# The table that orders all 831 steps, made anew with other lengths for TensorE's work

## The chip, the core and the metric

The kernel runs on one core of a Trainium2 chip. The metric is the device time of one execution in microseconds (us), the median over runs. A core has five instruction queues that run beside each other and wait for one another by semaphores: PE (TensorE, matrix products; its weight loads are listed apart as PEld), DVE (VectorE), ACT (ScalarE), POOL (GpSimd) and SP, which here only issues transfers. A product writes into PSUM, and DVE or ACT must take it out before the PSUM buffer can be used again.

## What is computed

The reference is a gated recurrence over 768 time steps for 4 x 8 heads of 40 values, and a gated feed-forward layer with a mixing over time behind it. Cut to what matters:

```python
def _attn_ref(q, k, v, i_gate, f_gate, o_gate):      # q, k, v, o_gate: 4 x 8 x 768 x 40
    for t in range(S):
        m_new = np.maximum(f_gate[:, :, t] + m, i_gate[:, :, t])
        f_stab = np.exp(f_gate[:, :, t] + m - m_new)
        i_stab = np.exp(i_gate[:, :, t] - m_new)
        m = m_new
        C = f_stab[:, :, None, None] * C + i_stab[:, :, None, None] * np.einsum('bhd,bhe->bhde', vt, kt)
        n = f_stab[:, :, None] * n + i_stab[:, :, None] * kt
        h_tilde = np.einsum('bhde,bhe->bhd', C, qt)
        denom = np.maximum(np.abs(np.einsum('bhd,bhd->bh', n, qt)[:, :, None]), 1.0)
        y[:, :, t] = h_tilde / denom / (1.0 + np.exp(-o_gate[:, :, t]))

def _moe_ref(x, w_in, w_spatial, b_spatial, w_out):  # x: 4 x 768 x 320
    h = np.maximum(x @ w_in, 0.0)
    u, v = h[..., :512], h[..., 512:]
    v_n = (v - v.mean(-1)) / np.sqrt(v.var(-1) + 1e-06)
    v_s = np.einsum('ts,bsd->btd', w_spatial, v_n) + b_spatial[None, :, None]
    return (u * v_s) @ w_out
```

## The kernel before

The recurrence is cut into 24 packs, n = 0 to 23: four batches b of six packs, each of 128 time steps and all eight heads. A pack needs five groups of PE products: `pe_ex` (L364, one product, the gates' exponents), `pe_s` (L370, keys by queries), `pe_dc` (L379, what the pack adds to the state), `pe_intra` (L387, values within the pack) and `pe_inter` (L396, the carried state by the queries). The last four are packs of small products, 16 in the program and 32 instructions in the trace, that use the array as four 64x64 tiles. They are called pack groups here.

Around them stand, on DVE: `keys` (L415, weights times `pe_s`, frees its PSUM), `step` (L433, or L431 at a batch's start: the state, twice a pack), `rows` (L441 reads what `pe_inter` wrote, L445 what `pe_intra` wrote), `norm` (L451 to L459, ends in the tile x); on ACT: `weights` (L401) and `gate` (L410, L412); on POOL: `ktw` (L406), `decay` (L423, the state before each step) and `gated` (L465, L467). Then `turn` (L478) transposes x on PE into px, and `turn_h` (L484, ACT) and `turn_l` (L490, DVE) split it into a high and a low part, xH and xL.

The feed-forward layer takes products with 128 rows, in three terms of high and low parts. They are called large products here. `a_v` (L528) makes one pv tile for each of a batch's six 128-step blocks, by eight products of 512 columns; `ln1`, `ln2`, `ln3` (L535 to L559, on ACT, DVE and POOL) normalise it into vH and vL. `b_pu` (L570, eight products) and `b_pb` (L579 to L581, 18 products) make pu and pb for each of eight parts of a batch, and `b_g1` (L587 to L593) combines them on DVE and ACT. `c_out` (L603 to L605) is the last product.

Weights arrive as 64-bit numbers. `conv` (L261 to L283) makes 14 pieces of them into high and low 32-bit parts with work on ACT, DVE and POOL, and `split` (L296, L298) does the like for the spatial weights, six halves on DVE and six on POOL. They are wanted by the large products, and their steps stand among the packs of the first batch.

The program builds a list `stages` of 831 generators in a plain order (packs, conversions, products). Each generator yields between its instructions. What order the instructions get on all five queues, and which PSUM and SBUF buffers follow each other, is set by a table of 2534 numbers: each number takes the next step of that generator.

```python
    gens = [steps(*s) for s in stages]
    for k in ORDER or [k for k in range(len(gens)) for _ in range(99)]:
        next(gens[k], None)
```

Each engine then works through its own queue in that order and never skips ahead of an instruction that waits. PSUM holds four buffers for ex, px, pv, pu, pb and pc in rotation, and one double buffer each for SX (`pe_s` and `pe_inter`) and DX (`pe_dc` and `pe_intra`).

Of the kernel before, what the change touches and what calls it, by code (L numbers as in the profile page):

```python
# [37 lines left out]
def mlstm_moe(ctx: ExitStack, tc: tile.TileContext, a):  # L38
# [806 lines left out]
    def steps(f, args):  # L845
        r = f(*args)
        if r is not None:
            yield from r
# [4 lines that stand above are left out]
# [73 lines left out]
```

## Time and profile before

| what | us |
|---|---|
| median of 3 runs | 376.23 |
| lowest and highest of them | 375.11, 378.67 |
| the profiled execution's own time | 378.9 |
| its span, first to last instruction | 377.1 |
| PE busy in the span | 330.6 |
| PE weight loads busy | 298.9 |
| DVE, ACT, POOL busy | 220.1, 144.8, 111.7 |

The profile's page cuts the span into 40 equal slices of 9.4 us and gives each engine's busy tenths, then lists groups of instructions and the waits behind them. A row of a timeline has start, duration, engine, source line, operation, output and input, and in brackets how long the engine stood idle before it and what ended that. Matmuls overlap: their durations are longer than the distance from one to the next, and the distance is what PE pays. In the rows for stretches, "PEclk" is the TensorE clock that was granted, as a share of full speed.

### The profile page before, as it was taken

The page shows a single profiled execution, that of the slowest core. Times are in us where ns is not written, and L with a number is a line of the kernel's source. Part 1 is how long each engine was busy: PE and PEld are TensorE (multiplying, and loading weights), DVE is VectorE, ACT ScalarE, POOL GpSimd, SP SyncE. Part 2 cuts the span into 40 slices and gives each one's busy share as a digit, 9 for nine tenths or more (in the row PEclk, how much of TensorE's full clock was granted, in tenths as well). Part 3 has the DMA queues.
Part 4 walks back from the last instruction along what each step waited for, and adds up shares of the span by engine and source line. Part 5 has one row for each costly group of instructions (what it writes and reads, how often), then busy time and mean ns, then how long its engine had stood idle before and what let it go on. Part 6 is the DMA issues. An engine that isn't in the chain of part 4 may idle for free.

```text
span 377.1 us, 10595 instructions
## 1 busy us (share of the span) xinstructions
PE 330.6 (88%) x4426; PEld 298.9 (79%) x4426; DVE 220.1 (58%) x552; ACT 144.8 (38%) x335; POOL 111.7 (30%) x178
## 2 busy tenths in 40 slices
PE   0215685989699999999999999999999999999996
PEld 0104574756678899989899999889899998999996
DVE  6556869569779877345767454447675234614231
ACT  6256214267624332367332322663321216701211
POOL 5156645256535244111423232123331101200000
PEclk9999999989869999999999999999999999999999
DMA  7856244554251324300233414002100100100101
GB/s 200 253 155 224 82 127 138 161 171 128 67 170 55 127 86 145 105 2 18 78 94 123 142 56 141 1 20 73 56 2 2 54 1 0 54 0 0 51 5 52
DMA packets 16047, 32.24 MB, mean 85 GB/s; under 512 B 4028, under 2 KB 8920, under 8 KB 16000
## 3 DMA queue, kind: packets, MB, share of 16 engines
q1 hardware_dynamic: 15456, 31.30, 27.3%
q8 instruction: 35, 0.57, 0.6%
q0 software_dynamic: 416, 0.15, 0.2%
q10 hardware_dynamic: 128, 0.12, 0.1%
q14 instruction: 12, 0.10, 0.1%
HBM read 27.19 MB, written 4.33 MB: 84 GB/s over the span
## 4 chain that ended last, share of the span: by engine, by line
PE 80%; DVE 7%; DMA 5%; POOL 3%; issue 2%; SPq 1%; ACT 1%; POOLq 0%; DVEq 0%; ACTq 0%
PE pv L528 12%; PE pu L570 12%; PE pb L579 10%; PE pb L581 9%; PE pb L580 9%; PE DX L387 4%; PE SX L396 4%; PE pc L603 4%; PE pc L605 4%; PE pc L604 4%; PE SX L370 3%; PE px L478 3%; DMA w<-in_w_in 2%; PE DX L379 2%; DMA QK<-in_qk 2%
## 5 line engine op out<-in xcount | busy, mean ns | idle before, releaser
L579 PE MATMUL pb<-wsH,vH 128*128 128x384 f32 x192 | 69.0, 359 | 0.7 <-DVE g L587 0.7
L580 PE MATMUL pb<-wsL,vH 128*128 128x384 f32 x192 | 65.2, 339 | 0.0
L581 PE MATMUL pb<-wsH,vL 128*128 128x384 f32 x192 | 65.0, 339 | 0.0
L591 ACT CAST big<-g 128x384 fp32r<-128x384 f32 x32 | 16.4, 513 | 95.3 <-DVE g L589 93.2
L587 DVE TENSOR_TENSOR g<-pb,bsp 128x384 f32<-128x384 f32 x32 | 17.8, 556 | 43.0 <-PE pb L581 42.7
L579 PEld LDWEIGHTS pb<-wsH,vH 128*128 128x128 f32 x192 | 36.3, 189 | 2.6 <-DVE g L587 1.0
L580 PEld LDWEIGHTS pb<-wsL,vH 128*128 128x128 f32 x192 | 36.5, 190 | 0.2
L581 PEld LDWEIGHTS pb<-wsH,vL 128*128 128x128 f32 x192 | 36.4, 190 | 0.0
L545 POOL TENSOR_TENSOR st<-st,half_neg 128x1 f32<-128x1 f32 x24 | 14.7, 619 | 67.5 <-DVE st L543 64.5
L570 PE MATMUL pu<-xH,wiH 128*128 128x384 f32 x96 | 33.1, 345 | 0.4 <-DVE xL L490 0.4
L423 POOL TENSOR_TENSOR ST<-ST,DEC 104x164 f32<-104x164 f32 x40 | 21.9, 548 | 37.5 <-DVE ST L433 24.7
L528 PE MATMUL pv<-wiH,xH 128*128 128x512 f32 x72 | 30.0, 428 | 0.0
L603 PE MATMUL pc<-woH,big 128*128 128x320 f32 x96 | 29.8, 311 | 0.0
L605 PE MATMUL pc<-woH,big 128*128 128x320 f32 x96 | 29.6, 308 | 0.0
L604 PE MATMUL pc<-woL,big 128*128 128x320 f32 x96 | 29.6, 308 | 0.0
L387 PEld LDWEIGHTS DX<-RH,KS 64*64 64x64 f32 x768 | 15.6, 154 | 13.8 <-DVE ST L433 7.6
L387 PE MATMUL DX<-RH,KS 64*64 64x41 f32 x768 | 18.6, 248 | 8.8 <-DVE ST L433 6.9
L401 ACT ACTIVATE W<-ex 128x512 f32<-128x512 f32 x24 | 14.3, 595 | 31.2 <-PE ex L364 19.0
L406 POOL TENSOR_TENSOR RH<-RH,W 128x320 f32<-128x320 f32 x24 | 17.7, 738 | 28.4 <-ACT W L401 27.7
L370 PE MATMUL SX<-QK 40*64 40x64 f32 x768 | 20.9, 258 | 5.1 <-DVE KS L415 4.7
L484 ACT ACTIVATE xH<-px 128x384 fp32r<-128x384 f32 x24 | 11.8, 490 | 34.4 <-PE px L478 34.3
L415 DVE TENSOR_TENSOR KS<-SX,W 128x512 f32<-128x512 f32 x24 | 16.5, 686 | 14.5 <-PE DX L387 9.5
(120 smaller groups left out, 766.3 us busy)
## 6 DMA issues: line engine op xcount, KB each, us to landing
RH<-in_vk SPq DMA_DIRECT2D x24, 484.0 KB
QK<-in_qk SPq DMA_DIRECT2D x48, 160.0 KB
out<-ot SPq DMA_DIRECT2D x24, 160.0 KB
big<-in_w_sp SPq DMA_DIRECT2D x6, 384.0 KB
w64b<-in_w_out SPq DMA_DIRECT2D x4, 320.0 KB
w<-in_w_in SPq DMA_DIRECT2D x4, 256.0 KB
w64b<-in_w_in SPq DMA_DIRECT2D x4, 256.0 KB
w<-in_w_rem SPq DMA_DIRECT2D x2, 256.0 KB
```

Source lines behind the costliest of these rows:

```text
L370: nc.tensor.matmul(s_[half(e ^ hf), hf, j * L:(j + 1) * L], QK[feat(hf), e, 0, j], QK[feat(hf), e, 1, j], start=True, stop=True)
L387: nc.tensor.matmul(intra_[half(e), hf, j * E:(j + 1) * E], ks[r, h], rh_v(rh)[r, h], start=True, stop=True)
L423: nc.gpsimd.tensor_tensor(out=ST[(2 * n + e + 1) % NST][0:HI], in0=state(n, e)[0:HI], in1=DEC[0:HI, 2 * k + e, b * HH:(b + 1) * HH].unsque ...
L528: nc.tensor.matmul(pm, l, r, start=i == 0, stop=i == len(terms) - 1)
L570: nc.tensor.matmul(pu, w, x, start=i == 0, stop=i == len(terms) - 1)
L579: nc.tensor.matmul(pb, vH[:, cd], wsH[hf][:, s], start=s == 0, stop=False)
L580: nc.tensor.matmul(pb, vH[:, cd], wsL[hf][:, s], start=False, stop=False)
L581: nc.tensor.matmul(pb, vL[:, cd], wsH[hf][:, s], start=False, stop=s == NB - 1)
L587: nc.vector.tensor_tensor(out=g, in0=pb_[(b, hf, d)], in1=bsp[:, hf * 384:hf * 384 + 384], op=ALU.add)
L603: nc.tensor.matmul(pc, gH[:, c], woH[:, d], start=d == 0, stop=False)
L604: nc.tensor.matmul(pc, gH[:, c], woL[:, d], start=False, stop=False)
L605: nc.tensor.matmul(pc, gL[:, c], woH[:, d], start=False, stop=d == 3)
```

## The change

Nothing but the table is different. The 831 stages, their code, their tiles and the number of instructions that do arithmetic stay as they are; the list is a new sequence of the same 2534 numbers. It was made with measured lengths of the pack groups in PE's two clock states, and of the changes between pack groups and large products. A line of it:

```diff
-ORDER = [5, 0, 0, 0, 16, 16, 2, 0, 4, 8, 9, 6, 28, 1, 7, 16, 18, 0, 42, 11, 3, 10, 14, 0, 18, 18, 12, 0, 20, 15,
...
+ORDER = [16, 16, 0, 0, 16, 0, 0, 1, 9, 3, 7, 4, 27, 0, 50, 18, 5, 13, 8, 0, 2, 12, 10, 0, 0, 18, 18, 15, 6, 20,
...
```

What it moves is seen in the queues. Three places on PE follow, before and after. In the names, SX and DX are the two PSUM buffers; the line tells the group. QK_108 and QK_109 hold the keys and queries of packs 6 and 7.

The first place is around packs 3 to 6. PE's queue before, from `pe_intra` of pack 3 to the first rows of `pe_inter` of pack 4:

```order
L387 MATMUL DX<-RH_105,KS_101 64x41 x16
L478 MATMUL px<-ident,x 128x128 x3
L364 MATMUL ex<-GM_76,AT_75 128x512
L379 MATMUL DX<-RH_103 40x41 x8
L387 MATMUL DX<-RH_102,KS_100 64x41 x16
L370 MATMUL SX<-QK_108 64x64 x16
L478 MATMUL px<-ident,x 128x128 x3
L396 MATMUL SX<-ST_114,QK_106 64x41 x2
```

The same place after:

```order
L379 MATMUL DX<-RH_102 40x41 x16
L387 MATMUL DX<-RH_105,KS_101 64x41 x16
L370 MATMUL SX<-QK_108 64x64 x16
L396 MATMUL SX<-ST_114,QK_106 64x41 x2
L396 MATMUL SX<-ST_115,QK_106 64x41 x2
```

`pe_s` of pack 6 and `pe_inter` of pack 4 moved ahead of two transposes, `pe_dc` of pack 5 and `pe_intra` of pack 4. On DVE, `keys` of pack 5, which frees SX for them, moved ahead of x of pack 3.

The second place is where the first large products begin. PE's queue before, from the end of the second pv tile:

```order
L528 MATMUL pv<-wiH,xL 128x512
L528 MATMUL pv<-wiH,xH 128x512
L528 MATMUL pv<-wiL,xL 128x512
L364 MATMUL ex<-GM_77,AT_75 128x512
L379 MATMUL DX<-RH_104 40x41 x16
L370 MATMUL SX<-QK_109 64x64 x16
L387 MATMUL DX<-RH_103,KS_101 64x41 x16
```

The same groups after, in the first pv tile:

```order
L528 MATMUL pv<-wiH,xH 128x512
L370 MATMUL SX<-QK_109 64x64 x16
L528 MATMUL pv<-wiL,xH 128x512
L528 MATMUL pv<-wiH,xL 128x512
L528 MATMUL pv<-wiH,xH 128x512
L528 MATMUL pv<-wiL,xL 128x512
L379 MATMUL DX<-RH_104 40x41 x16
L396 MATMUL SX<-ST_111,QK_107 64x41 x2
```

`pe_s` of pack 7 and `pe_dc` of pack 6 moved from behind both pv tiles to within and behind the first one, ahead of `pe_inter` of pack 5. Four products of the second tile then stand ahead of `pe_intra` of pack 5, and four behind it.

The third place is around `pe_intra` of pack 7 (DX from RH_105). PE's queue before:

```order
L364 MATMUL ex<-GM_77,AT_73 128x512
L570 MATMUL pu<-xH,wiL 128x384
L570 MATMUL pu<-xL,wiH 128x384
L570 MATMUL pu<-xH,wiH 128x384
L570 MATMUL pu<-xL,wiL 128x384
L379 MATMUL DX<-RH_102 40x41 x16
L387 MATMUL DX<-RH_105,KS_101 64x41 x16
L396 MATMUL SX<-ST_115,QK_109 64x41 x2
```

The same place after:

```order
L528 MATMUL pv<-wiL,xL 128x512
L379 MATMUL DX<-RH_102 40x41 x16
L579 MATMUL pb<-wsH_93,vH 128x384
L580 MATMUL pb<-wsL_95,vH 128x384
L581 MATMUL pb<-wsH_93,vL 128x384
L387 MATMUL DX<-RH_105,KS_101 64x41 x16
L579 MATMUL pb<-wsH_93,vH 128x384
L580 MATMUL pb<-wsL_95,vH 128x384
```

Three products of the first pb tile moved in between `pe_dc` of pack 8 and `pe_intra` of pack 7, and `pe_inter` of pack 7 moved ahead of both.

2 lines of the change are left out of this document (1 added, 1 removed).

## The prediction, made before the changed kernel ran

> **What bounds the kernel now.** I read the page's slices first, then the stretches, then who waits for whom, then the timeline at the places where a wait is long.
>
> ```profile
> PE   0215685989699999999999999999999999999996
> DVE  6556869569779877345767454447675234614231
> ```
>
> PE is full from the twelfth slice on (9.4 us each, so from about 112 us) and half empty before. DVE is busiest in the slices where PE is not full. The stretches say it in numbers; columns are span, PE, PE weight loads, DVE, ACT, POOL, granted clock, DMA share, GB/s:
>
> ```profile
> 30.70:62.20 31.50, 21.19 (x590) 17.77 (x590) 24.51 (x57) 12.12 (x28) 18.00 (x27) 1.00 0.44 131
> 62.20:77.60 15.40, 14.41 (x228) 10.96 (x228) 8.27 (x23) 4.54 (x11) 4.30 (x7) 1.00 0.47 142
> 77.60:83.30 5.70, 3.93 (x72) 2.93 (x72) 4.30 (x14) 4.49 (x13) 3.79 (x6) 0.70 0.70 229
> 83.30:96.50 13.20, 12.85 (x147) 9.64 (x143) 12.60 (x31) 9.52 (x25) 8.68 (x13) 1.00 0.33 92
> 96.50:100.30 3.80, 0.70 (x45) 0.58 (x46) 3.49 (x11) 2.02 (x4) 1.95 (x4) 1.00 0.28 51
> 100.30:110.60 10.30, 10.30 (x207) 9.12 (x204) 5.96 (x18) 4.48 (x11) 3.73 (x7) 0.50 0.48 150
> 110.60:112.00 1.40, 1.40 (x9) 1.24 (x8) 1.40 (x3) 0.00 (x0) 1.07 (x1) 1.00 0.77 302
> 112.00:370.00 258.00, 256.92 (x3080) 239.69 (x3080) 140.92 (x359) 90.81 (x206) 57.14 (x92) 1.00 0.18 55
> ```
>
> The reader is to see two regimes. From 112 to 370 us PE is busy 256.92 of 258.00 us at full clock: only less PE work helps there. From 30.7 us (the first `keys`) to 112.0 us (the end of the first pb tile) PE and DVE take turns waiting. DVE is busy 24.51 + 8.27 + 4.30 + 12.60 + 3.49 + 5.96 + 1.40 = 60.5 of 81.3 us, idle 20.8. PE runs part of the time at half clock: 0.50 in 100.3 to 110.6. The clock of 1.00 shown before 77 us is not to be believed, since the products themselves are slow there:
>
> ```profile
> 75.13 0.63 PE L528 MATMUL pv<-wiH,xH 128*128 128x512 f32 x1
> 75.56 0.63 PE L528 MATMUL pv<-wiL,xL 128*128 128x512 f32 x1
> 84.30 0.39 PE L528 MATMUL pv<-wiH,xH 128*128 128x512 f32 x1
> 84.53 0.40 PE L528 MATMUL pv<-wiL,xH 128*128 128x512 f32 x1
> ```
>
> Starts are 0.43 us apart at 75 us and 0.23 at 84. So PE is at half clock until about 76.5 us; these are its two states.
>
> **The marker.** Both tables put exactly the same PE work ahead of the 18th and last product of the first pb tile: packs up to `pe_s` of 10 and `pe_dc` of 9, six pv tiles, two pu tiles. Before, that product ends at 112.0 us. Since PE never waits behind it, the change is worth the shift of this marker, plus what PE's work behind it gains or loses.
>
> **Term 1, conversions come earlier: +4.7 us on DVE.** Ahead of the first `b_g1`, DVE now has more `conv` work: about two further pieces of w_out. Their rows:
>
> ```profile
> L272 DVE SCALAR_TENSOR_TENSOR bitsb<-w64b,bitsb 128x320 f32<-128x320 uint32 x4 | 3.2, 803 | 0.0
> L263 DVE TENSOR_SCALAR bitsb<-bitsb 128x320 int32<-128x320 int32 x4 | 2.8, 696 | 0.0
> L265 DVE SCALAR_TENSOR_TENSOR bitsb<-w64b,bitsb 128x320 int32<-128x320 int32 x4 | 2.0, 497 | 0.0
> L283 DVE TENSOR_TENSOR woL<-bitsb 128x320 fp32r<-128x320 f32 x4 | 1.9, 478 | 0.0
> L270 DVE TENSOR_SCALAR bitsb<-bitsb 128x320 int32<-128x320 int32 x4 | 1.3, 320 | 0.0
> ```
>
> Twice (0.80 + 0.50 + 0.48 + 0.32) and once 0.70 is 4.9 us, less 0.2 for a `rows` that now follows and a `step` that now precedes: 4.7. This work isn't new, it leaves the stretch behind the marker, where DVE has room (140.92 of 258). Bounds: 0 if all of it falls into DVE's idle time, 4.7 if none does; I count it in full and the idle time apart. The splits and the later w_in pieces move further, from between packs 5 to 8 to between packs 2 to 5, but stay on the same side of the marker.
>
> **Term 2, DVE's waits: -10.5 us.** What DVE waited for between 30.7 and 112.3 us, the four longest:
>
> ```profile
> DVE xs L441 <- PE SX L370: 6.3, 2, 4.7
> DVE x L459 <- PE px L478: 2.6, 2, 2.2
> DVE KS L415 <- PE SX L396: 2.5, 1, 2.5
> DVE KS L415 <- PE DX L387: 1.9, 2, 1.1
> ```
>
> (a) The 2.5 us are `keys` of pack 6, held up by `pe_inter` of pack 4 behind a transpose:
>
> ```profile
> 65.82 0.90 PE L478 MATMUL px<-ident,x 128*128 128x128 f32 x3
> 66.65 1.09 PE L396 MATMUL SX<-ST,QK 40*64 40x41 f32 x32
> 67.91 0.69 DVE L415 TENSOR_TENSOR KS<-SX,W 128x512 f32<-128x512 f32 x1 [2.46 <-PE SX L396]
> ```
>
> In the new queue `pe_inter` of pack 4 stands four groups earlier, and `keys` waits for `pe_intra` of pack 4 alone. Bounds 0 to -2.5; I take -2, since the waits for `pe_intra` in the list are about 1 us at most and partly there already.
>
> (b) The 4.7 us are `rows` of pack 5. `pe_inter` of pack 5 was done early, but DVE was kept from SX until `pe_s` of pack 7, which stood behind the second pv tile:
>
> ```profile
> 71.38 1.09 PE L396 MATMUL SX<-ST,QK 40*64 40x41 f32 x32
> 76.87 0.67 PE L370 MATMUL SX<-QK 40*64 40x64 f32 x32
> 77.60 0.50 DVE L441 TENSOR_TENSOR xs<-SX,ET 128x328 f32<-128x328 f32 x1 [4.67 <-PE SX L370]
> ```
>
> Now `pe_s` of pack 7 stands ahead of `pe_inter` of pack 5. What is late next: that `pe_inter` stands behind half a pv tile (four products of 0.43 us, 1.7 us), and x of pack 5 behind the rest of the second tile and a transpose. Bounds 0 to -4.7; I take -2.5.
>
> (c) The worst stall of PE comes after the clock has risen:
>
> ```profile
> 96.51 0.52 PE L379 MATMUL DX<-RH 64*40 64x41 f32 x32
> 99.76 0.31 DVE L433 TENSOR_TENSOR ST<-DX,ST 104x164 f32<-104x164 f32 x1
> 100.12 0.95 PE L387 MATMUL DX<-RH,KS 64*64 64x41 f32 x32 [3.10 <-DVE ST L433]
> ```
>
> `pe_intra` of pack 7 waited 3.10 us for the first `step` of pack 8, which stood in DVE's queue behind the normalisation of three blocks. Behind this gap the clock fell to 0.50 for 10.3 us. PE was the bound there: DVE idled 10.30 - 5.96 = 4.3 us. The new order puts three pb products into the gap, and has the normalisations earlier in DVE's queue against PE, because (a) and (b) bring DVE forward. I expect a gap of about 1 us, and no fall. The 4.3 us then go to about 1: -3.5 (bounds 0 to -4.3).
>
> (d) In 30.7 to 62.2 us DVE idled 31.5 - 24.5 = 7.0 us in many short waits. The pieces and splits moved in between the packs fill some: -2.5 (bounds 0 to -7.0).
>
> Together -2 - 2.5 - 3.5 - 2.5 = -10.5, half of the 20.8.
>
> [...]
>
> **Term 3, changes on PE behind the marker: -0.7 us.** What a pack group costs among large products:
>
> ```profile
> 120.86 0.34 PE L581 MATMUL pb<-wsH,vL 128*128 128x384 f32 x1
> 121.13 0.68 PE L387 MATMUL DX<-RH,KS 64*64 64x41 f32 x32
> 121.74 0.44 PE L579 MATMUL pb<-wsH,vH 128*128 128x384 f32 x1
> 122.02 0.33 PE L580 MATMUL pb<-wsL,vH 128*128 128x384 f32 x1
> 122.19 0.34 PE L581 MATMUL pb<-wsH,vL 128*128 128x384 f32 x1
> ```
>
> Large products start 0.17 apart (122.02 to 122.19). Entering takes 0.27 and the first product behind takes 0.28, so about 0.1 + 0.1 are lost at each end of a run, and up to 0.1 more inside. Behind the marker the old queue has 29 runs of pack groups between large products, the new one 27, and four fewer places where a transpose adjoins a group: 2 x 0.2 to 0.3 plus 4 x about 0.05, say -0.7. So little, because lengths and changes were already roughly served.
>
> **What else moves.** SP now issues the last three transfers of spatial weights ahead of those for RH of pack 5, instead of at 73 us; at 131 GB/s used in that stretch against 229 in a later one there is room, and I cost it at nothing. If not, `ktw` of pack 5 is late next. POOL gets two splits ahead of `decay` of pack 4; POOL's 18.00 of 31.50 us leave room, and its cost is nothing unless that `decay` is late for `step`.
>
> **The sum.** 4.7 - 10.5 - 0.7 = -6.5 us. On the profiled execution, 378.9, that is 372.4; on the median, 376.23, it is 369.7. The profiled one lies 2.7 above the median, perhaps with a longer fall of the clock than others, which would make (c) smaller for them; the choices in (a) to (d) lie in the middle of their bounds. I predict 369.7.
>
> **Rivals.**
> - More of the waiting goes: the bounds of (a) to (d) add up to -18.5; if -15.5 of it goes, 376.2 + 4.7 - 15.5 - 0.7 = 364.7. For it: all three long waits lose their cause at once. Against: each has a next one behind it.
> - The waits only change place: DVE idles as long as the added work is, so -4.7, and the marker stays: 376.2 - 0.7 = 375.5. For it: PE and DVE depend on each other at every group, and the half clock slows both. [...]
> - DVE is the bound, and the conversions delay the state. If none of DVE's 20.8 us of idle time goes, the marker is 4.7 us later: 376.2 + 4.7 - 0.7 = 380.2, slower. For it: DVE is busy 12.60 of 13.20 us in 83.3 to 96.5. Against: its longest wait had nothing to do with DVE's load. It decides from an idle time that shrinks by less than 4.0 us.
>
> **How the numbers follow.** A measurement of this kernel can tell about 1% from no change. The forecast has a chance of 0.45 (366.5 to 372.5), the first rival 0.18, the second 0.24, the third 0.13. Faster by over 1% (below 372.5): 0.63. Within 1%: 0.25. Slower: 0.12. The range from 363.5 to 377.0 leaves out about 2 in 10, on the rivals' far sides.
>
> **What would show it.** The last product of the first pb tile ends at about 105.5 us (before 112.0). `rows` of pack 5 waits under 3 us. No stall of PE above 2 us between 84 us and the marker, and no half clock there. DVE idles about 10 us between the first `keys` and the marker. Behind it PE stays busy over 99%, with 27 runs. I am wrong if the marker is at 110 or later, if the clock falls once more, or if PE waits for DVE behind the marker.

## The result, and the profile after

The changed kernel takes 364.24 us (median of 4 runs, 364.11 to 364.68), the kernel before, run beside it, 375.67 us (4 runs, 374.69 to 378.67). The ratio is 0.9685, with a 95% interval of 0.9628 to 0.9742. The profiled execution of the changed kernel took 364.34 us, its span is 362.5. The forecast was 369.7 in a range of 363.5 to 377.0: the sign is right, the size is that of the first rival (364.7).

The page's slices (9.1 us each) of the changed kernel, PE, DVE and the granted clock:

```profile
PE   1123764999999999999999999999999999999996
DVE  6668999799988861447587273565844435533131
PEclk9999999999999999999999999999999999999999
```

PE is full from the eighth slice on, before from the twelfth. In slices 4 to 14 DVE's digits are 8 or 9 but for one 7; before they went down to 5. PEclk counts the time before the trace's first clock record as full speed, which it isn't: products of 512 columns start 0.42 us apart at 70.25 us and 0.23 apart at 72.34.

For the stretches I cut both kernels at the same work: first `keys`, first product of the first pv tile, the marker (last product of the first pb tile), last products. Columns as in the prediction: span, then busy time of PE, PE weight loads, DVE, ACT and POOL, granted clock, DMA share, GB/s. The stretches of the kernel before:

```profile
0.00:30.74 30.74, 5.15 (x44) 3.50 (x44) 17.69 (x42) 15.03 (x38) 13.07 (x26) 1.00 0.74 216
30.74:67.67 36.93, 25.73 (x705) 21.64 (x705) 27.72 (x64) 13.97 (x32) 20.90 (x31) 1.00 0.45 133
67.67:112.16 44.49, 39.21 (x578) 30.60 (x574) 32.94 (x88) 23.18 (x58) 20.63 (x29) 0.85 0.45 137
112.16:374.00 261.84, 260.48 (x3104) 243.15 (x3103) 141.79 (x360) 92.38 (x210) 57.14 (x92) 1.00 0.17 54
```

The same stretches of the changed kernel:

```profile
0.00:31.13 31.13, 5.25 (x44) 3.51 (x44) 20.75 (x49) 17.52 (x44) 13.79 (x27) 1.00 0.76 221
31.13:69.67 38.54, 26.03 (x705) 21.73 (x706) 34.51 (x74) 15.70 (x35) 24.69 (x35) 1.00 0.53 165
69.67:99.80 30.13, 29.98 (x576) 23.36 (x574) 28.56 (x82) 19.70 (x50) 16.30 (x24) 1.00 0.46 138
99.80:360.00 260.20, 259.16 (x3104) 243.20 (x3103) 139.82 (x350) 91.60 (x208) 56.88 (x92) 1.00 0.18 56
```

The marker moved from 112.16 to 99.80 us, 12.36 earlier. All of that comes from one stretch, from the first pv tile to the marker: 44.49 us became 30.13. The packs ahead of it even take 1.61 us longer (36.93, 38.54). In the stretch that gained, PE idled 5.28 us before and 0.15 after (span less busy time), which is 5.13 of the 14.36 us; the other 9.23 is the same work done in less busy time, 29.98 us in place of 39.21. The clock can account for all of it. Before, PE was at half clock there until 76.46 and in two falls later:

```profile
76.46:79.87 3.41, 1.58 (x97) 1.37 (x96) 2.04 (x5) 3.17 (x8) 1.97 (x3) 1.00 0.49 147
79.87:83.28 3.41, 3.41 (x52) 2.40 (x44) 2.26 (x9) 2.22 (x7) 2.03 (x4) 0.50 0.73 247
96.94:100.35 3.41, 0.31 (x26) 0.23 (x16) 3.10 (x10) 1.69 (x3) 1.56 (x3) 1.00 0.30 56
100.35:103.76 3.41, 3.41 (x99) 3.29 (x92) 1.80 (x4) 2.48 (x7) 1.68 (x3) 0.50 0.32 129
```

These are windows of 3.41 us. Behind a window in which PE idled 1.83 us (3.41 - 1.58) follows one at 0.50; behind one with 3.10 us idle follow three (to 110.59). In the changed kernel the products of the first pv tile show when the clock rises, and no record shows it falling before the end:

```profile
70.25 0.63 PE L528 MATMUL pv<-wiL,xH 128*128 128x512 f32 x1
72.34 0.39 PE L528 MATMUL pv<-wiH,xL 128*128 128x512 f32 x1
```

Full speed begins at 70.98 by the trace's clock records, 1.31 us behind the start of that tile (69.67); before, it was 8.79 us (67.67 to 76.46). So 8.79 + 13.65 = 22.4 us at half clock became 1.3. Half of the difference, 10.6 us (an estimate, by the products' starts of 0.42 and 0.23 us apart), bounds what the clock can have given; 9.23 were seen.

The waits of DVE, 31 to 100 us, of the changed kernel (total, times, longest):

```profile
DVE x L459 <- PE px L478: 1.9, 2, 1.7
DVE KS L415 <- ACT W L401: 1.1, 2, 0.6
DVE KS L415 <- PE DX L387: 0.6, 2, 0.4
```

The wait of `rows` for `pe_s` (6.3 us before) is gone from the list. From the first `keys` to the marker DVE idles 38.54 - 34.51 + 30.13 - 28.56 = 5.60 us, before 9.21 + 11.55 = 20.76.

Not all went well. PE's waits from 31 to 360 us in the changed kernel begin with one of 5.3 us, and PE's longest wait behind the first `keys` was 3.1 before:

```profile
PE SX L370 <- DVE KS L415: 6.2, 2, 5.3
PE DX L379 <- POOL RH L406: 4.7, 1, 4.7
```

DVE and POOL at the place of the 5.3 us, changed kernel (start, duration):

```profile
59.46 3.44 DVE L272 SCALAR_TENSOR_TENSOR bitsb<-w64b,bitsb 128x256 f32<-128x256 uint32 x1
62.83 0.49 DVE L445 TENSOR_TENSOR xs<-DX,xs 128x328 f32<-128x328 f32 x1
63.24 0.68 DVE L415 TENSOR_TENSOR KS<-SX,W 128x512 f32<-128x512 f32 x1
59.42 1.01 POOL L298 TENSOR_TENSOR wsL<-big,wsH 128x384 fp32r<-128x384 f32 x1
60.37 0.88 POOL L467 TENSOR_TENSOR x<-RH,x 128x320 f32<-128x320 f32 x1
61.18 0.76 POOL L406 TENSOR_TENSOR RH<-RH,W 128x320 f32<-128x320 f32 x1
61.88 0.74 POOL L280 TENSOR_TENSOR bitsb<-bitsb,wiH 128x256 f32<-128x256 f32 x1
```

A step of conv 8 (L272) that takes 0.42 us in other places took 3.44, just while POOL worked without a break, and `rows` and `keys` of the next packs stood behind it. This is the change's own new cost, and it lies in the stretch that got longer.

### The profile page after: what moved, and what is told of

It is laid out like the page before. It is cut to its first block, busy times and chain, and to the rows that moved or that the text cites. A ratio compares the mean times of both kernels' runs of the same rounds, so it can differ in the third digit from the quotient of the medians.

```text
span 362.5 us, 10599 instructions
## 1 busy us (share of the span) xinstructions
PE 320.4 (88%) x4426; PEld 291.8 (80%) x4426; DVE 223.7 (62%) x552; ACT 144.5 (40%) x335; POOL 111.7 (31%) x178
## 4 chain that ended last, share of the span: by engine, by line
PE 77%; DMA 8%; DVE 7%; issue 3%; ACT 2%; POOL 1%; SPq 1%; ACTq 0%; DVEq 0%; POOLq 0%
PE pu L570 12%; PE pv L528 10%; PE pb L579 10%; PE pb L581 9%; PE pb L580 9%; PE pc L603 4%; PE pc L605 4%; PE pc L604 4%; DMA QK<-in_qk 4%; PE DX L387 3%; PE SX L396 3%; PE SX L370 3%; PE px L478 2%; DMA RH<-in_vk 2%; PE DX L379 2%
## 5 line engine op out<-in xcount | busy, mean ns | idle before, releaser
L579 PE MATMUL pb<-wsH,vH 128*128 128x384 f32 x192 | 67.8, 353 | 0.2 <-DVE g L587 0.2
L370 PE MATMUL SX<-QK 40*64 40x64 f32 x768 | 20.1, 250 | 15.4 <-DMA QK<-in_qk 8.0
L370 PEld LDWEIGHTS SX<-QK 40*64 40x64 f32 x768 | 16.6, 159 | 18.2 <-DMA QK<-in_qk 8.2
L528 PE MATMUL pv<-wiH,xH 128*128 128x512 f32 x72 | 28.7, 408 | 0.1
L593 DVE TENSOR_TENSOR big<-g,big 128x384 fp32r<-128x384 f32 x32 | 18.6, 581 | 12.3 <-ACT big L591 12.3
L406 POOL TENSOR_TENSOR RH<-RH,W 128x320 f32<-128x320 f32 x24 | 18.8, 781 | 19.0 <-ACT W L401 18.7
L465 POOL TENSOR_TENSOR x<-RH,x 128x64 f32<-128x64 f32 x24 | 9.1, 380 | 48.4 <-DVE x L459 45.5
```

The source lines that it names most:

```text
L370: nc.tensor.matmul(s_[half(e ^ hf), hf, j * L:(j + 1) * L], QK[feat(hf), e, 0, j], QK[feat(hf), e, 1, j], start=True, stop=True)
L406: nc.gpsimd.tensor_tensor(out=kt, in0=kt, in1=Wt[n][:, :, L - 1:L].broadcast_to([128, H, D]), op=ALU.mult)
L528: nc.tensor.matmul(pm, l, r, start=i == 0, stop=i == len(terms) - 1)
L579: nc.tensor.matmul(pb, vH[:, cd], wsH[hf][:, s], start=s == 0, stop=False)
L593: nc.vector.tensor_tensor(out=gL, in0=g, in1=gH.bitcast(F32), op=ALU.subtract)
```

## The experiments

Four questions: which part of the list brings the gain (e1, e2); whether single waits of the kernel before explain it (e3 to e6); what a stall costs in the changed kernel (e12); and whether the 3.44 us and DVE's load ahead of the first pv tile are real costs (e7 to e11). All were timed beside the kernel before, whose medians in the four sessions were 377.68, 377.43, 377.64 and 376.33 us.

| run | median us | ratio to before, 95% |
|---|---|---|
| e1_new_head | 368.50 | 0.9665 to 0.9798 |
| e2_new_tail | 378.29 | 0.9963 to 1.0056 |
| e3_s7_earlier | 377.36 | 0.9943 to 1.0016 |
| e4_step8_earlier | 375.67 | 0.9916 to 0.9985 |
| e5_step8_block2 | 373.93 | 0.9856 to 0.9927 |
| e6_both_stalls | 374.33 | 0.9876 to 0.9944 |
| e7_conv8_later | 361.64 | 0.9530 to 0.9607 |
| e8_convs_one_back | 362.49 | 0.9559 to 0.9622 |
| e9_two_back_splits | 364.75 | 0.9620 to 0.9727 |
| e10_one_back_splits | 363.78 | 0.9597 to 0.9681 |
| e11_one_back_w0 | 363.53 | 0.9589 to 0.9678 |
| e12_held_step8 | 368.96 | 0.9775 to 0.9850 |

**The head or the tail of the list.** "old" and "new" are the two lists.

```diff
-ORDER = new
+ORDER = new[:558] + [the numbers still left, in the sequence of old]     # e1_new_head
-ORDER = old
+ORDER = old[:547] + [the numbers still left, in the sequence of new,     # e2_new_tail
+                      but the steps of conv(10) to conv(13) at later places]
```

> The list of the changed kernel up to the last product of the first pb tile, then the rest in the order of before. Theory (nearly all of the gain lies ahead of that product, as the two profiles say: 112.16 against 99.80 us, and 2.2 us behind it): 366.4 us (365.3 to 367.5), the tile ends at 99.8 +- 0.5, the clock stays at 1.0 from 71 us on. Rival (the order behind the marker carries a good part, the 27 runs in place of 29 and the transposes): 368 us or more.

> The list of before up to the last product of the first pb tile, then the rest in the changed order (the w_out pieces that the changed list had done by then stand among it). Theory: 375.7 - 2.2 = 373.5 us (372.3 to 375.2), the tile still ends at about 112 us, the clock still falls to 0.50 behind the stall of pe_intra 7. Rival (order behind the marker carries a good part): 371 us or less.

In e1 the marker came at 100.02 us, as in the changed kernel, so the head alone brings the whole shift. But three of its four runs took 368.46 to 368.62 us at a mean clock of 0.994 or 0.995, and one took 365.81 at 1.00. The profile is of the former kind:

```profile
100.02:103.43 3.41, 1.93 (x39) 1.63 (x39) 2.48 (x7) 1.54 (x3) 1.62 (x3) 1.00 0.40 104
103.44:106.85 3.41, 3.41 (x13) 3.41 (x12) 1.52 (x7) 0.00 (x0) 0.46 (x1) 0.50 0.33 127
```

Just behind the marker the old tail has PE wait 1.48 us for DVE's g, and the next window is at half clock. The run without a fall lies in the theory's 365.3 to 367.5, the median 1 us above it: I had not reckoned with a fall at the seam.

e2 missed: 378.29 us in place of 373.5. It isn't the new tail alone, since 16 steps of conversions that the new list has ahead of the marker must come behind it. In its profile PE idled 3.38 us there. The busy time still tells something. Behind the marker PE was busy 260.48 us with the old tail (before) and 259.16 with the new (after). In e2, with the new one, it is 259.74 (263.12 to the last product less the 3.38), in e1, with the old one, 260.21 (263.42 less 1.50 idle and less 1.71, half a window, for the clock). So the new order behind the marker is worth 0.5 to 1.3 us of busy time; the two spans differ by 2.24 us there (377.1 - 112.16 = 264.94 and 362.5 - 99.80 = 262.70), and 0.8 of the rest is idle time (1.08 before, 0.29 after).

**The single waits.** e3 moves one PE group of the kernel before (names as in the excerpts above: QK_109 is pack 7's):

```diff
 L528 MATMUL pv<-wiH,xH 128x512
+L370 MATMUL SX<-QK_109 64x64 x16
 L396 MATMUL SX<-ST_111,QK_107 64x41 x2
...
 L379 MATMUL DX<-RH_104 40x41 x16
-L370 MATMUL SX<-QK_109 64x64 x16
 L387 MATMUL DX<-RH_103,KS_101 64x41 x16
```

> Before with one move: pe_s of pack 7 ahead of pe_inter of pack 5, as in the changed kernel. Rival A (each wait costs its length): DVE's wait of 4.67 us of rows 5 goes and the marker comes 3 to 4.7 us earlier, 371 to 372.7 us. Theory (what counts is the stall of pe_intra 7 and the fall of the clock behind it): the wait goes, yet PE has the same pv tiles to do and DVE the same normalisations ahead of step 8.0, the stall and the fall stay, and the time is 373.5 to 376 us.

The theory held. DVE's 4.67 us are gone, and the time is the same (377.36). Rows of e3, DVE and then PE:

```profile
72.94 0.49 DVE L441 TENSOR_TENSOR xs<-SX,ET 128x328 f32<-128x328 f32 x1
76.32 0.15 DVE L543 TENSOR_SCALAR st<-st 128x1 f32<-128x1 f32 x1 [2.89 <-ACT vL L537]
77.66 0.68 PE L387 MATMUL DX<-RH,KS 64*64 64x41 f32 x32 [2.32 <-DVE ST L431]
```

`rows` of pack 5 now starts 4.7 us earlier than before, but DVE's next instruction waits 2.89 us for a normalisation, and PE's stall at `pe_intra` 5 is 2.32 us in place of 1.83.

e4 takes the stall that I had blamed most, e5 besides exchanges two blocks' normalisations, e6 mends the stall at `pe_intra` 5 as well:

```diff
 pe_dc(8)
+step(8, 0)
+keys(8)
...
-step(8, 0)
...
-keys(8)
# e5, besides: the places of ln2, ln3 of block 2 and of block 3 exchanged
# e6, besides: pe_s(7) ahead of pe_inter(5); pe_dc(6) ahead of the second half of a_v(0, 1);
#              step(6, 0) right behind the first half of rows(5)
```

> Before with one move: the first step of pack 8 and keys of pack 8 stand right behind pe_dc of pack 8 in the list, so on DVE ahead of the normalisations that held them. Theory (the stall of 3.10 us and the 10.24 us at half clock behind it are most of the gain): the stall is under 1.5 us, no fall behind it, the half clock's 5.1 us and about 2 us of the stall go, less 1 us of normalisation that pb products then wait for: 369.6 us (368 to 371.5). Rival (DVE bounds that stretch, the fall costs little because PE would wait for DVE anyway): 373.5 to 375.5 us.

> Before with the first step and keys of pack 8 right behind pe_dc of pack 8 (the run e4_step8_earlier), and besides the places of the normalisations of blocks 2 and 3 exchanged, so that block 2, which the third group of the first pb tile reads, is normalised ahead of blocks 3 and 4. Theory (every window of 3.41 us in which PE idled 1.40 us or more was followed by half clock, and none with 0.91 or less; in e4_step8_earlier it was 0.45 us at pe_intra 7 and 1.78 us at that pb group): the 1.78 us go to under 0.7 us, no fall at 95 to 110 us; about 5 us of half clock's loss and 1 us of idle time go against e4_step8_earlier: 370 us (368 to 372). Rival (the fall costs little, since PE would wait for DVE at full clock): 374 to 376 us.

> The run e5_step8_block2 with the stall at pe_intra 5 mended too: pe_s of pack 7 ahead of pe_inter of pack 5, pe_dc of pack 6 ahead of the second half of the second pv tile, and the first step of pack 6 right behind the first half of rows 5 on DVE. Theory: the stall of 1.83 us and the single window at half clock behind it (3.41 us) go as well, clock 1.0 from the first rise on, another 2.5 to 3.5 us: 367 us (365 to 369.5), that is most of the changed kernel's gain with none of its other moves. Rival (the other moves carry it): no lower than 372 us.

e4 gave 2.0 us by the medians (377.68, 375.67), where 6 were expected. PE's waits at the place in e4:

```profile
95.15 0.68 PE L387 MATMUL DX<-RH,KS 64*64 64x41 f32 x32 [0.45 <-DVE ST L433]
98.69 0.69 PE L579 MATMUL pb<-wsH,vH 128*128 128x384 f32 x1 [1.78 <-ACT vH L557]
```

The 3.10 us became 0.45 and 1.78, and the clock fell all the same, behind a window with 1.40 us of idle time and for 10.24 us from 97.85. In e5 the 1.78 us are down to 0.7, yet PE still idles by small amounts:

```profile
94.44:97.85 3.41, 2.75 (x99) 2.07 (x99) 3.05 (x10) 1.21 (x3) 1.39 (x3) 1.00 0.43 114
97.86:101.27 3.41, 2.40 (x68) 1.76 (x69) 3.10 (x8) 3.33 (x9) 2.12 (x4) 1.00 0.39 136
101.27:104.68 3.41, 3.41 (x42) 2.90 (x42) 2.68 (x10) 1.16 (x3) 1.36 (x3) 0.50 0.80 206
```

A window with 0.66 us idle was followed by full clock, one with 1.01 us by half clock, now for one window and not three. e5 is 3.5 us under before (377.43), but missed as well: 373.93 lies above the forecast 368 to 372, just under the rival's 374 to 376. As the fall stayed in e4 and e5, neither tells what it costs. e6 missed outright (374.33 against 367, the rival's "no lower than 372" held): its stall at `pe_intra` 5 went, and the transposes of the same pack waited as long for POOL. PE's waits of e6 from 66 to 110 us, and its two windows about the second fall:

```profile
PE px L478 <- POOL x L467: 1.8, 1, 1.8
```

```profile
97.10:100.51 3.41, 2.63 (x79) 1.81 (x71) 2.73 (x9) 1.72 (x4) 0.61 (x2) 1.00 0.59 181
100.51:103.92 3.41, 3.04 (x68) 2.28 (x67) 3.41 (x13) 2.72 (x8) 2.68 (x4) 0.50 0.22 67
```

Even 0.78 us of idle time sufficed there. What follows from e3 to e6: no one of the old list's waits carries the gain. Where one is mended PE waits at the next place, and in all four profiles the clock still fell twice. The new list left 0.15 us of idle time in 30 us, and the clock did not fall. Whether a stall there brings a fall is what e12 tests.

**What a stall costs in the changed kernel.**

```diff
 def step(n, e):
...
+        if (n, e) == (8, 0):
+            idle = wk.tile([128, 256], F32, name="idle", tag="idle", bufs=1)
+            for _ in range(10):
+                nc.vector.memset(idle, 0.0)
```

> The changed kernel with ten fillings of an otherwise unused tile (128x256) put on DVE ahead of the first step of pack 8, 2 to 2.8 us by DVE's operations of that size, so that pe_intra of pack 7 is held as it was before the change. Theory (a stall there costs itself and, in a window of 3.41 us, the clock behind it): PE idles about 2 us in one window, the next window or the next three are at 0.50, and the time is 364.2 + 2 + 1.7 to 5.1 = 368 to 371.5 us. Rival (a stall costs its length only): 366 to 367 us. Or DVE catches up unseen: 364.2 to 365 us.

The fillings took 3.80 us, more than expected. DVE and PE of e12, where lines behind the added code are four higher, then the three windows:

```profile
91.16 3.80 DVE L433 MEMSET idle<- 128x256 f32 x10
95.20 1.09 PE L387 MATMUL DX<-RH,KS 64*64 64x41 f32 x32 [3.65 <-DVE ST L437]
```

```profile
90.58:93.99 3.41, 0.97 (x30) 0.60 (x17) 2.57 (x12) 2.12 (x6) 0.00 (x0) 1.00 0.22 84
93.99:97.40 3.41, 2.20 (x36) 2.13 (x37) 2.83 (x9) 0.00 (x0) 1.61 (x3) 0.50 0.00 0
97.40:100.81 3.41, 3.41 (x12) 3.31 (x11) 2.11 (x5) 0.60 (x1) 1.90 (x4) 0.50 0.41 120
```

One stall of 3.65 us brought two windows at half clock. From the first pv tile to the marker it took 36.28 us in place of 30.13: 6.15 more, of which 3.57 is idle time and the rest the clock's (half of 2.20 + 3.41 is 2.8). The median is 4.7 us above the changed kernel's; the profiled run's first pv tile came 1.2 us earlier than in the changed kernel's profile, which accounts for most of the difference. So between these two points the stall cost its length and 70% more (6.15 for 3.57). By its length alone, the rival, the time would be 364.2 + 3.65 = 367.9; the four runs took 368.50 to 369.87. They were timed in another session than the changed kernel, so the medians alone are a weak witness; the fall in the profile is the strong one. It comes with this one stall, in a kernel that otherwise has none.

**The cost that the change brought, and DVE's load.** e7 moves one conversion step of the changed kernel on DVE, e8 shifts conversions:

```diff
 L433 TENSOR_TENSOR ST_111<-DX,ST_111 104x164
+L445 TENSOR_TENSOR xs<-DX,xs 128x328
+L415 TENSOR_TENSOR KS_101<-SX,W 128x512
 L272 SCALAR_TENSOR_TENSOR bitsb<-w64b,bitsb 128x256
-L445 TENSOR_TENSOR xs<-DX,xs 128x328
-L415 TENSOR_TENSOR KS_101<-SX,W 128x512
# e8: conv(8) at the places of conv(9) in the list, conv(9) at those of conv(10), and so on to conv(12);
#     conv(13) 113 to 183 numbers behind the marker; load_w(10) to load_w(13) behind what frees their buffers
```

> The changed kernel with one move: the piece of conv 8 that DVE held for 3.44 us at 59.46 (0.42 us elsewhere) while POOL worked without a break goes behind rows 3 and keys 5 in DVE's queue, and what depends on it with it. Theory (an operation of DVE with two operands in SBUF gives way to POOL's, one that reads PSUM doesn't): PE's wait of 5.29 us for keys 5 falls to about 2 us, the first pv tile and the marker come 1.5 to 3 us earlier: 362 us (361 to 363.3). Rival (the packs of that stretch are held by DVE's whole load, or the next such piece is held in its place): 363.8 to 365 us.

> The changed kernel with every piece of conv 8 to 12 at the places where those of the next one stood (conv 13 behind), so that about 2.3 us of DVE's conversions leave the stretch ahead of the marker. Theory (DVE bounds the packs up to 70 us: 29.3 us busy of 32 in 28 to 60): the first pv tile and the marker come 1 to 2.5 us earlier, 362.5 us (361.5 to 363.5). Rival (what the pieces took was idle time, so that term 1 of the prediction, +4.7 us, was none): 364 to 365 us. Or a wait for a late load of weights costs more than it brings: above 365.5 us.

By the medians both came as the theory has it: 361.64 and 362.49 us against 364.24, which was timed in another session. The step of e7 in its new place:

```profile
58.70 0.68 DVE L415 TENSOR_TENSOR KS<-SX,W 128x512 f32<-128x512 f32 x1
59.30 2.46 DVE L272 SCALAR_TENSOR_TENSOR bitsb<-w64b,bitsb 128x256 f32<-128x256 uint32 x1
```

`keys` of pack 5 starts at 58.70 in place of 63.24, the step itself is still slow beside POOL (2.46), and PE's longest wait for `keys` fell from 5.3 to 1.7 us. From the first `keys` to the first pv tile it took 36.23 us in place of 38.54; 36.48 in e8. Nearly half of e7's gain is not the edit's. In the profiles e7's marker comes 2.73 us earlier than the changed kernel's (97.07, 99.80), and 1.30 of that lies ahead of the first `keys` (29.83, 31.13), where the two lists are alike; in e8 it is 1.06 of 2.91. In the profiles that share this opening (all with the new head but e11) the first `keys` come between 29.62 and 31.13. So from the first `keys` to the marker e7's edit is worth 1.4 us: 2.3 ahead of the first pv tile, less 0.9 behind it (31.01 in place of 30.13). e7 is the fastest of all kernels here, by the medians 0.7% under the changed one.

e9 to e11 tried for more and missed:

```diff
# e9: conv(8), conv(9) at the places of conv(10), conv(11); conv(10) to conv(13) behind the marker;
#     split(0, 1), split(2, 1), split(4, 1) from between packs 3 to 5 to between the pv tiles
# e10: e8, and those splits to between packs 6 to 8 and the pv tiles
# e11: e8, and pe_ex(0), pe_ex(1), weights(0), keys(0), ktw(0) ahead of the last pieces of conv(4) and conv(5)
```

> The changed kernel with conv 8 and 9 at the places of conv 10 and 11, conv 10 to 13 behind the marker, and the twelve steps of the second half's splits moved from between packs 3 to 5 to between the pv tiles (some 77 to 95 us). Theory (up to the first pv tile DVE is the bound, and it also loses time to POOL's splits there; behind it PE and DVE are both full, but DVE has been relieved of two pieces): keys of pack 0 to the first pv tile 33 us in place of 38.5, the marker 2 us earlier than in e8_convs_one_back, 360.5 us (359 to 362). Rival (DVE becomes the bound between the pv tiles, or the pieces behind the marker hold up the first large products there): 363 to 367 us.

> The run e8_convs_one_back with the second half's splits moved to between packs 6 and 8 and the pv tiles, the conversions as they were in it. Theory (POOL's splits next to DVE's cost DVE 2 to 3 us ahead of the first pv tile, 0.56 + 0.89 + 0.54 us of its own splits there besides a wait of 2.2 us for one): the first pv tile 2 us earlier, the marker 1 us: 361.5 us (360.3 to 362.5). Rival (moved, the splits take from DVE between the pv tiles what they gave ahead of them, where DVE has 2 us free in 30): 362.5 to 364 us.

> The run e8_convs_one_back with the first weights, keys and scaled K of pack 0 ahead of the last pieces of conv 4 and 5 on ACT, DVE and POOL (PE waits 3.7 to 4.7 us there for the scaled K). Theory (the chain of packs starts up to 3 us earlier, but DVE has the same work up to the first pv tile and is busy 31.5 of 36.5 us): the wait goes to under 1.5 us, and 0.5 to 1.5 us of it reach the marker, 361.5 us (360.8 to 362.3). Rival (the chain bounds, not DVE's load): 359.5 to 360.5 us. Or the pieces that now come later hold up the first pack: 362.5 us or more.

They took 364.75, 363.78 and 363.53 us. The two stretches of e10:

```profile
30.32:65.11 34.79, 26.03 (x705) 21.73 (x706) 28.02 (x66) 12.75 (x28) 20.85 (x32) 1.00 0.62 193
65.11:98.12 33.01, 31.19 (x576) 23.70 (x574) 31.05 (x85) 22.16 (x55) 18.94 (x27) 1.00 0.47 135
```

Without the splits the packs come 1.7 us faster to the first pv tile than in e8 (34.79, 36.48), and behind it more than that is lost again (33.01, 30.34): PE idles 1.82 us there, which it didn't in e8, and is busy 0.85 us longer. In e9 the same happened (34.80 and 32.04), and its pieces behind the marker cost PE 2.1 us of waits. In e11 PE's wait for the first scaled K fell from 3.7 to 1.1 us, and the displaced pieces made `keys` of pack 1 late by 3.8. DVE's work must be somewhere, and the changed list's places for the splits are near the best of those tried.

## Why the prediction was right, and where it was not

- **The frame.** The forecast is 5.5 us off and its range held, at its lower end. The marker carries the change: yes, 12.36 of the 14.6 us between the spans, and e1 gets the same marker from the head alone. PE stays full behind it: 259.16 of 260.20 us. It ends at 99.80, not at 105.5. In the prediction's own account, from the first `keys` on: DVE's added work 2.4 and its idle time -15.2, where 4.7 and -10.5 were forecast, so term 1 was 2.3 us too large and term 2 4.7 too small.
- **Term 1, +4.7.** Nearly right in size, not in place. DVE's work up to the marker grew from 17.69 + 27.72 + 32.94 = 78.35 to 83.82 us, 5.5 more, but 3.06 of that lies ahead of the first `keys` (20.75 less 17.69). Between it and the marker it is 2.4, and 3.0 of that stretch is the slow step of conv 8 (3.44 less 0.42).
- **Term 2, -10.5.** DVE's idle time fell by 20.76 - 5.60 = 15.2 us, the first rival's 15.5. (a) did not bring its 2 us: `keys` of pack 6 starts at 69.33 and not 67.91, behind the slow step. (b) The wait went wholly, but e3 shows that this alone is worth nothing. (d) is right in direction: ahead of the first pv tile DVE's idle time went from 9.2 to 4.0 us.
- **The step that failed is (c)** and the way it was priced. I counted the half clock by DVE's idle time, 4.3 us, in one fall only. The row with clock 0.70 from 77.6 to 83.3 stood in my own fence and got no term, nor did the late rise to full clock at 76.5. Between the first pv tile and the marker PE was busy 9.2 us longer before, with 22.4 us at half clock in place of 1.3, and all of that went. I also took the 3.10 us stall for the cause of the fall. e4 brings that stall down to 0.45 us and the clock falls at the same place; e4 to e6 show falls from 0.78 to 1.83 us of idle time.
- **Term 3, -0.7.** In the two profiles it is 2.24 us: 0.8 of waiting that I had not counted, 1.3 of busy time (260.48 less 259.16), and 0.5 to 1.3 by e1 and e2. The size of the busy part was about right.
- **Costed at nothing.** The transfers of SP: right, PE waited for no weights there. POOL's splits: wrong. They did not make `decay` late. One of them is the first of the four POOL operations beside DVE's slow step, and moving that step gets back 1.4 us up to the marker (e7).
- **Rivals.** Waits that only change place: this is what happens when one is mended alone (e3, e6), not with the whole list. DVE as the bound: ahead of the first pv tile nearly so, 34.51 of 38.54 us, and there the kernel did get slower, by 1.61 us.

Why the new list succeeds where e6 fails isn't settled wait by wait. What it does is seen: DVE does its conversions in time that it idled away ahead of the first pv tile, and behind it no group of PE is kept waiting.

## What to carry to other kernels

Price a stall of PE by its length and by the half clock behind it (6.15 us for 3.57 of idle time in e12). In a stretch of small and large products, 0.78 to 1.83 us of idle time in a window brought such falls in e4 to e6, and mending them one by one gained little as long as others were left. Before moving side work into an engine's idle time, look whether another engine is busy then: beside POOL's work a DVE step of 0.42 us took 3.44 here. And give every row with a lowered clock a term of its own in the sum.

## What the runs showed of the hardware

**The clock.** In the traces its records change only at steps of 3.41 us (before: at 76.46, 79.87, 83.28, 100.35 and 110.59). In the profiles of before, the changed kernel and e1 to e12 there are 14 falls between the first rise and the last products; each stands behind a window with 0.78 to 3.10 us of PE's idle time, and every window at full clock with 1.40 us or more was followed by one. Between 0.78 and 1.28 it goes both ways. The largest idle time without a fall is in e2, the columns as above:

```profile
137.16:140.57 3.41, 2.13 (x14) 1.84 (x13) 3.27 (x7) 0.70 (x2) 1.99 (x3) 1.00 0.47 144
```

So 1.28 us did no harm with 14 products in the window, 10 of them large; 0.78 (e6) and 1.01 (e5) did with 79 and 68, nearly all of the small kind that packs are made of. Nine falls lasted one window, two lasted two and three lasted three. Two windows of the kernel before, within one fall, are both wholly busy; the first was followed by half clock, the second by full:

```profile
103.76:107.17 3.41, 3.41 (x69) 2.85 (x69) 3.26 (x13) 0.95 (x2) 1.33 (x2) 0.50 0.26 78
107.17:110.59 3.42, 3.42 (x41) 2.91 (x41) 0.84 (x2) 1.00 (x2) 0.67 (x2) 0.50 0.86 242
```

It is so in all the falls: of their 19 wholly busy windows the five with 69 products or more kept half clock, the 14 with 60 or fewer ended it. Ahead of the first rise, 17 windows (counted back from it in steps of 3.41 us) were wholly busy without one large product, and none was followed by full clock. That small products count for less than large ones is a guess that fits these rows (69 and more against 60 and fewer); no run tried it by itself. The list alone doesn't set the length of a fall: before and e2 have the same list up to the marker, and their second fall lasted three windows in the one and one in the other. Why the first rise in the profile before took 8.79 us, with wholly busy windows in it that held five and seven large products, stays open. By these rows a partly idle window can be enough for a fall (0.78 of 3.41 us in e6; the 1.28 of e2 was not), and a wholly busy one doesn't always end it (five of 19 did not).

**DVE beside POOL.** From 28 to 110 us in the changed kernel (minimum, median and longest in ns, first and last start; the step of conv up to 70 us):

```profile
L272 DVE SCALAR_TENSOR_TENSOR bitsb<-w64b,bitsb x3: 374/416/3444, 44.0 to 59.5; 128x256 f32<-128x256 uint32 x3
L441 DVE TENSOR_TENSOR xs<-SX,ET x10: 482/490/491, 36.8 to 108.0; 128x328 f32<-128x328 f32 x10
L415 DVE TENSOR_TENSOR KS<-SX,W x11: 676/691/692, 31.1 to 105.6; 128x512 f32<-128x512 f32 x11
```

Operations that take one operand from PSUM (L441, L415) kept their time to 3% beside POOL; over all profiles none of their 672 is more than 3% above its median. Some with both operands in SBUF stretched (in brackets the median in the changed kernel): L272 to 3.44 us (0.42), in the kernel before L298 to 2.25 (0.55) at 84.31 and L265 to 2.23 (0.42) at 41.71. Operations with a single SBUF operand stretched too: L270 to 1.52 (0.29) at 35.13 in the changed kernel and L451 to 1.30 (0.16) at 60.69 in e8. All five lay beside POOL operations that followed each other without a break. The step of 3.44 us ran from 59.46 to 62.90, beside the four POOL operations from 59.42 to 62.62 (1.01, 0.88, 0.76 and 0.74 us). My theory in e7 goes by the number of operands in SBUF. It fits L272, L298 and L265 on the one side and L441 and L415 on the other, and says nothing of L270 and L451; why an operation stretches was not shown.
